# Seven half-size products in the first layer of a fused retention and MLP kernel, with two output buffers and two units cast sooner

## The chip, the cores and the metric

The kernel runs on one core of one Trainium2 chip. The metric is the device time of one launch in microseconds, lower is better. A version is compared with the kernel before in the same rounds on the same chip. The ratio given for it is the mean time of its fast runs over the mean time of the other's fast runs of the same rounds, so it isn't quite the ratio of the two medians that stand beside it.

## The reference

```python
def _attn_ref(q, k, v):                      # (8, 8, 576, 64) each, float32
    B, H, S, D_ = q.shape
    scores = (1.0 / np.sqrt(D_)) * np.matmul(q, k.transpose(0, 1, 3, 2))
    gamma = 1.0 - 2.0 ** (-5.0 - np.arange(H, dtype=np.float32))
    rel = np.arange(S)[:, None] - np.arange(S)[None, :]
    Dmat = np.where(rel >= 0, gamma[:, None, None] ** rel[None, :, :], 0.0)
    return np.matmul(scores * Dmat[None], v).astype(np.float32)

def _moe_ref(x, w_in, w_out):                # x (4608, 512), w_in (512, 2048), w_out (2048, 512)
    h = x @ w_in
    return (np.maximum(0.01 * h, h) @ w_out).astype(np.float32)
# reference: x is the attention output, heads side by side; the result is _moe_ref(x)
```

## The kernel before

Tokens come in 36 units of 128, and four units form a group of 512 (nine groups). A unit is loaded, cast (k on ScalarE, q and v with their decays on GpSimd), transposed by DMA, and turned into a piece of x by small matmuls ("scores", "outputs") and VectorE sums. A group then runs through two dense layers on TensorE. The second layer of groups 1 to 8 is already done as seven half-size products in place of eight, with the sums ("mix") on VectorE. The attention work of the next group is laid between the matmuls of this one. The code is shortened, and the comments are added for this text.

```python
    o_pool = ctx.enter_context(tc.tile_pool(name="op", bufs=3))      # output rows, 4 KB a partition each
    acc_pool = ctx.enter_context(tc.tile_pool(name="accp", bufs=4, space=PSUM))
    # ...
    def h_mm(hps, n, g, f, ts):
        for c in range(NP):                                          # NP = 4
            nc.tensor.matmul(out=hps[:, n, :], lhsT=w_in16[:, c, f * P : (f + 1) * P],
                             rhs=xT[g][:, c, ts], start=(c == 0), stop=(c == NP - 1))
    def h_block(g, f):                                               # one of 16 first-layer blocks of a group
        hps = acc_pool.tile([P, 1, TOK], FP, name="acc")             # TOK = 512
        h_mm(hps, 0, g, f, slice(0, TOK))
        leaky(g_tile(g)[:, f : f + 1, :], hps)                       # ScalarE
    def store(g, a, osb):
        nc.sync.dma_start(out=..., in_=osb)                          # SyncE's queue, as all later loads
    # second layer of group 0: wide(tb, part), one store half way, one at its end; of groups 1 to 8:
        plan = (
            ("p1", g_part(g, 0, 0), w_part(0, 0), True, lambda: keep("k1", "p1")),
            ("p1", g_part(g, 0, 1), w_part(1, 0), False, lambda: give(0, 0, "p1")),       # ScalarE
            ("p6", s[:, 1], w_mix[:, 1], True, lambda: keep("u2", "p6", "k1")),
            ("p5", s[:, 0], w_mix[:, 0], True, lambda: keep("v", "p5", "u2")),
            ("p7", g_part(g, 1, 0), w_mix[:, 2], True, lambda: give(1, 1, "p7", "v")),    # VectorE
            ("p5", g_part(g, 0, 0), w_part(1, 1), False, lambda: give(0, 1, "p5", "u2")), # VectorE
            ("p7", g_part(g, 1, 1), w_mix[:, 3], False, lambda: give(1, 0, "p7", "u2")),  # VectorE
        )
        # hooks after a product: 0 and 4 hold one step each
    # ...
    def burst(u, out=True):
        scores(u); outputs(u - 1)                                    # TensorE
        masks(u); state(u, 0); state(u, 1)                           # VectorE
        state_cast(u, pool_copy)                                     # GpSimd
        own(u - 1); add(u - 1)                                       # ScalarE, VectorE: a piece of x
    def ahead(u):
        cast_k(u)                                                    # ScalarE
        cast_q(u, nc.gpsimd); cast_v(u, nc.gpsimd)                   # GpSimd
        transpose_dma(u)                                             # SyncE's queue
    def step(u):
        burst(u); load(u + 4); ahead(u + 2)
```

Of the kernel before, what the change touches and what calls it, by code (L numbers as in the profile page):

```python
# [9 lines left out]
FP = mybir.dt.float32  # L10
F16 = mybir.dt.float16
MUL = mybir.AluOpType.mult
ADD = mybir.AluOpType.add
SUB = mybir.AluOpType.subtract
# [4 lines left out]
def kernel(  # L19
# [9 lines left out]
    nc = tc.nc  # L29
# [3 lines left out]
    P = 128  # L33
    CH = 64
    BLK = 256
    NP = H // 2
# [5 lines left out]
    HF, HN, HT = NF // 2, DM // 2, TOK // 2  # L42
# [11 lines left out]
    for w, at in enumerate(kinds):  # L54
        r = np.concatenate([CH * a + np.arange(CH) for a in at])[:, None] - BLK / 2
# [13 lines left out]
    const_pool = ctx.enter_context(tc.tile_pool(name="const", bufs=1))  # L69
# [3 lines left out]
    x_pool = ctx.enter_context(tc.tile_pool(name="xp", bufs=3))  # L73
    g_pool = ctx.enter_context(tc.tile_pool(name="gp", bufs=2))
    s_pool = ctx.enter_context(tc.tile_pool(name="sp", bufs=1))
    o_pool = ctx.enter_context(tc.tile_pool(name="op", bufs=3))
    m_pool = ctx.enter_context(tc.tile_pool(name="mp", bufs=1))
    sc_pool = ctx.enter_context(tc.tile_pool(name="scp", bufs=1, space=PSUM))
    ot_pool = ctx.enter_context(tc.tile_pool(name="otp", bufs=1, space=PSUM))
    acc_pool = ctx.enter_context(tc.tile_pool(name="accp", bufs=4, space=PSUM))  # L80
# [23 lines left out]
    w_in16 = const_pool.tile([P, NP, DFF], F16, name="w_in16")  # L104
    w_out16 = const_pool.tile([P, NF, DM], F16, name="w_out16")
    w_mix = const_pool.tile([P, 4, HF, HN], F16, name="w_mix")
    zst = const_pool.tile([P, NP, CH], F16, name="zst")
    idle = const_pool.tile([P, TOK], F16, name="idle")

    t32, qk16, v16, qkT, s16s, st16, sc_tiles, ot_tiles, xT = ({} for _ in range(9))  # L110
# [8 lines left out]
    def load(u, eng=None, after=None):  # L119
        for x in (1, 0, 2):  # L120
            t = ld_pool.tile([P, H, D], FP, name=f"t32_{x}")
            t32[u, x] = t
            c = 2 * u
            same = c % CB + 1 < CB
            e = eng[x] if isinstance(eng, dict) else eng or nc.sync
            engs = e if isinstance(e, tuple) else (e,)
            n = H // len(engs)
            for j, rows in ((0, P),) if same else ((0, CH), (1, CH)):
                b, w = (c + j) // CB, (c + j) % CB
                for i, e in enumerate(engs):  # L130
                    hs = slice(n * i, n * i + n)
                    d = e.dma_start(
                        out=t[CH * j : CH * j + rows, hs],
                        in_=(q, k, v)[x][b, hs, CH * w : CH * w + rows, :].rearrange(
                            "h t d -> t h d"
                        ),
                    )
                    if after is not None and (x in after or not isinstance(after, dict)):
                        behind(d, *(after[x] if isinstance(after, dict) else after))
                        after = None  # L140
                    last_load[u, x] = d
# [24 lines left out]
    def decay(u, x):  # L166
        w = kinds.index((place(2 * u), place(2 * u + 1)))
        return tab_sb[:, w, x, :].unsqueeze(2).to_broadcast([P, H, D])
# [5 lines left out]
    def cast_q(u, eng):  # L174
        eng.tensor_tensor(out=qk16[u][:, 0], in0=t32[u, 0], in1=decay(u, 0), op=MUL)  # L175

    def cast_v(u, eng):
        v16[u] = a_pool.tile([P, H, D], F16, name="v16")
        eng.tensor_tensor(out=v16[u], in0=t32[u, 2], in1=decay(u, 1), op=MUL)  # L179
# [54 lines left out]
    def masks(u):  # L234
        s16s[u] = b_pool.tile([P, 2, NP, CH], F16, name="s16")
        nc.vector.tensor_tensor(  # L236
            out=s16s[u],
            in0=sc_tiles[u][:, :, 0],
            in1=mask_sb.unsqueeze(1).unsqueeze(1).to_broadcast([P, 2, NP, CH]),
            op=MUL,  # L240
        )
# [3 lines left out]
    def state(u, j):  # L245

        if j == 0:
            s32s[u] = a_pool.tile([P, 2, NP, CH], FP, name="s32")
            st16[u] = a_pool.tile([P, 2, NP, CH], F16, name="st16")
        c = (2 * u + j) % CB  # L250
        if c == CB - 1:
            carry[0] = None
            return
        st = sc_tiles[u][:, j, 1]
        to = s32s[u][:, j]
        scaled = c % (BLK // CH) == BLK // CH - 1
        if carry[0] is None:
            nc.vector.tensor_copy(out=to, in_=st)
        elif not scaled:
            nc.vector.tensor_tensor(out=to, in0=st, in1=carry[0], op=ADD)  # L260
        else:
            tmp = m_pool.tile([P, NP, CH], FP, name="stmp")
            nc.vector.tensor_tensor(out=tmp, in0=st, in1=carry[0], op=ADD)
            nc.vector.tensor_tensor(  # L264
                out=to, in0=tmp,
                in1=gblk_sb.unsqueeze(2).to_broadcast([P, NP, CH]), op=MUL,
            )
        carry[0] = to
# [4 lines left out]
    def state_cast(u, copy, js=(0, 1)):  # L273
        js = [j for j in js if live(u, j)]
        if len(js) == 2:
            copy(out=st16[u], in_=s32s[u])  # L276
        else:
            for j in js:
                copy(out=st16[u][:, j], in_=s32s[u][:, j])  # L279
# [107 lines left out]
    def g_tile(g):  # L387
        if g not in g_t:
            g_t[g] = g_pool.tile([P, NF, TOK], F16, name="gt")
        return g_t[g]  # L390

    def leaky(out, in_):
        nc.scalar.activation(out=out, in_=in_, func=mybir.ActivationFunctionType.Lrelu)  # L393

    def h_block(g, f):
        hps = acc_pool.tile([P, 1, TOK], FP, name="acc")
        h_mm(hps, 0, g, f, slice(0, TOK))
        leaky(g_tile(g)[:, f : f + 1, :], hps)
# [8 lines left out]
    def h_unit(u, fb):  # L407
        g, t0 = u // 4, (u % 4) * P
        ts = slice(t0, t0 + P)
        hps = acc_pool.tile([P, 4, P], FP, name="acc")  # L410
        for n in range(4):
            h_mm(hps, n, g, 4 * fb + n, ts)
        leaky(g_tile(g)[:, 4 * fb : 4 * fb + 4, ts], hps)



# [29 lines left out]
    def mix_weights(n, x):  # L446
        fs = slice(x * HF // 2, (x + 1) * HF // 2)
        a, b = (
            (w_part(0, 1), w_part(0, 0)),
            (w_part(1, 1), w_mix[:, 0]),  # L450
            (w_part(1, 1), w_part(0, 1)),
            (w_part(1, 0), w_mix[:, 1]),
        )[n]
        nc.vector.tensor_tensor(out=w_mix[:, n, fs], in0=a[:, fs], in1=b[:, fs], op=SUB)
# [111 lines left out]
    pool_copy, act_copy, dve_copy = nc.gpsimd.tensor_copy, nc.scalar.copy, nc.vector.tensor_copy  # L566
# [82 lines left out]
    def halves(g, *items):  # L649
        for a, fb in items:  # L650
            h_half(g, a, fb)

    def cast_qv(u):
        cast_q(u, nc.vector)
        cast_v(u, nc.vector)
# [5 lines left out]
    def settle(u):  # L661
        state(u, 0)
        state_cast(u, dve_copy, (0,))
        masks(u)
        state(u, 1)
# [11 lines left out]
    def mixes(g, *ns):  # L677
        for n in ns:
            mix(g, n, 0)
            mix(g, n, 1)  # L680
# [16 lines left out]
    def ahead(u):  # L697

        if u >= NU:
            return  # L700
        cast_k(u)
        cast_q(u, nc.gpsimd)
        cast_v(u, nc.gpsimd)
        transpose_dma(u)
# [5 lines left out]
    def step(u):  # L710
        burst(u)
        fetch(u + 4)
        ahead(u + 2)
# [37 lines left out]
    turn(6, 0)  # L751
    h_unit(5, 0)
    scores(6)
    settle(6)
    cast_qv(7)
    h_unit(5, 1)
    turn(7, 1)
    halves(1, (0, 4))
# [15 lines left out]
    mix_weights(0, 0)  # L774
    mix_weights(0, 1)
    h_unit(7, 0)
    h_unit(7, 1)
    mix_weights(1, 0)
    mix_weights(1, 1)
    halves(1, (1, 4))  # L780
    load(10)
    ahead(8)
    mix_weights(2, 0)
    mix_weights(2, 1)
    halves(1, (1, 5), (1, 6))
    ahead(9)
    load(11)
    mix_weights(3, 0)
    mix_weights(3, 1)
    halves(1, (1, 7))  # L790

    def early(u, n):
        burst(u)
        ahead(n)
        load(n + 2)
# [4 lines left out]
        3: lambda: mixes(1, 1),  # L800
        4: lambda: (burst(8, False), ahead(11), load(13)),
        7: lambda: mixes(1, 2),
        9: lambda: early(9, 12),
    }
    for n in range(16):
# [1 line left out]
        if n in at:  # L807
            at[n]()
    burst(10)
    seven(1, {0: [lambda: early(11, 13)], 4: [lambda: early(12, 14)]})  # L810

    first = [f for i in range(4) for f in (i, i + HF)]
    second = [f for i in range(4, 8) for f in (i, i + HF)]
    for g in range(2, NG):
        more = g < NG - 1
        for n, f in enumerate(first + second):
            h_block(g, f)
            if more and n in (4, 12):
                step(4 * g + 5 + (n == 12))
            if n == 8:  # L820
                for m in range(3):
                    mix(g, m, 0)
        for m in range(3):
            mix(g, m, 1)
        seven(
            g,
            {0: [lambda: step(4 * g + 7)], 4: [lambda: step(4 * g + 8)]} if more else {},
            g == NG - 1,
        )

# [29 lines left out]
```

## Time and profile before

| | before |
|---|---|
| median of three runs | 289.74 us (288.94 to 289.91) |
| span of the profiled execution | 288.4 us |
| TensorE busy | 279.5 us, 97% |
| VectorE, ScalarE, GpSimd busy | 172.8, 143.7, 104.2 us |
| one steady group (groups 3 to 6) | 29.1 us, TensorE never idle |

In the profile a group of instructions is named by its line, engine, operation and its tile "out<-in". TensorE is what bounds this kernel, so its listed idle time, and what ended it, says whether another engine costs anything. In groups 2 to 8 of this kernel no such wait is listed.

### The profile page before, as it was taken

What the parts mean: (1) busy time and instruction counts of PE and PEld (TensorE: products, weight loads), DVE (VectorE), ACT (ScalarE), POOL (GpSimd) and SP (SyncE); (2) the same over time, 40 slices, a digit from 0 to 9 for tenths busy, and PEclk for the clock granted to TensorE, in tenths of its full rate; (3) what the DMA queues carried; (4) which work ended last, traced back from release to release, by engine and by line L of the source; (5) the groups of instructions that cost most, each with busy time, mean ns of one, the idle gap of its engine ahead of it and who ended that gap; (6) DMA issues with size and microseconds to landing.
All of it is one profiled execution on the core that took longest, in us unless ns stands there. A gap on an engine that the chain in (4) does not pass through costs nothing.

```text
span 288.4 us, 9432 instructions
## 1 busy us (share of the span) xinstructions
PE 279.5 (97%) x4111; PEld 190.5 (66%) x4111; DVE 172.8 (60%) x297; ACT 143.7 (50%) x254; POOL 104.2 (36%) x124
## 2 busy tenths in 40 slices
PE   8799999989999999999999999999999999999994
PEld 3478889545874587458745874587458844884583
DVE  2874787974664595459545863586368636740352
ACT  4676766623237632773277327732773176317610
POOL 8969503654333334332434333234225413000000
PEclk9999999999999999999999999999999999999999
DMA  8999999899999997976896669766986151012003
GB/s 221 297 228 203 293 207 213 187 195 212 217 254 283 210 212 164 277 148 148 183 256 152 146 153 285 148 144 152 283 159 147 45 177 39 3 65 84 0 2 145
DMA packets 131738, 50.01 MB, mean 173 GB/s; under 512 B 121264, under 2 KB 126000, under 8 KB 131696
## 3 DMA queue, kind: packets, MB, share of 16 engines
q1 hardware_dynamic: 125392, 39.59, 59.5%
q0 software_dynamic: 6016, 9.70, 15.0%
q8 instruction: 32, 0.52, 0.7%
q10 hardware_dynamic: 288, 0.11, 0.1%
q14 instruction: 10, 0.08, 0.1%
HBM read 36.81 MB, written 9.44 MB: 160 GB/s over the span
## 4 chain that ended last, share of the span: by engine, by line
PE 87%; DMA 6%; DVE 3%; ACT 2%; issue 1%; SPq 0%; POOL 0%; POOLq 0%
PE acc L379 41%; PE acc L493 34%; PE acc L429 3%; PE sc L218 3%; DMA t<-in_k_dram 2%; DMA t<-in_q_dram 2%; PE ot L294 2%; DMA qkT<-qk 2%; PE sc L227 1%; PE ot L305 1%; PE acc L200 1%; ACT qkT L207 1%; PE acc L327 1%; DVE s L236 0%; DVE xT L366 0%
## 5 line engine op out<-in xcount | busy, mean ns | idle before, releaser
L379 PE MATMUL acc<-xT,w_in 128*128 128x512 f16 (+2 forms) x768 | 131.0, 326 | 0.3 <-ACT xT L347 0.2
L393 ACT ACTIVATE gt<-acc 128x512 f16<-128x512 f32 x144 | 85.9, 597 | 56.9 <-PE acc L379 55.5
L379 PEld LDWEIGHTS <-w_in 128*128 128x128 f16 x768 | 68.2, 98 | 51.7 <-issue 0.2
L493 PEld LDWEIGHTS <-gt 128*128 128x128 f16 x640 | 61.8, 98 | 9.1
L236 DVE TENSOR_TENSOR s<-sc,cs 128x512 f16<-128x512 f32 x34 | 23.3, 686 | 39.7 <-PE sc L227 39.7
L493 PE MATMUL acc<-w_out,gt 128*128 128x256 f16 x384 | 45.9, 273 | 0.2
L276 POOL CAST st<-s 128x512 f16<-128x512 f32 x21 | 12.8, 609 | 89.7 <-DVE s L260 56.3
L361 ACT COPY own<-ot 128x512 f32<-128x512 f32 x33 | 19.3, 585 | 42.8 <-PE ot L305 35.6
L175 POOL TENSOR_TENSOR qk<-t,cs 128x512 f16<-128x512 f32 x28 | 29.9, 1067 | 19.4 <-DMA t<-in_q_dram 19.0
L473 DVE TENSOR_TENSOR mix<-gt 128x1024 f16<-128x1024 f16 x16 | 15.7, 984 | 28.8 <-ACT gt L393 28.8
L179 POOL TENSOR_TENSOR v<-t,cs 128x512 f16<-128x512 f32 x28 | 31.9, 1139 | 1.2 <-DMA t<-in_v_dram 1.2
L493 PE MATMUL acc<-w_mix,gt 128*128 128x256 f16 x256 | 30.6, 273 | 0.0
L493 PE MATMUL acc<-w_mix,mix 128*128 128x256 f16 x256 | 29.6, 273 | 0.0
L493 PEld LDWEIGHTS <-mix 128*128 128x128 f16 x256 | 25.0, 98 | 3.1 <-DVE mix L473 0.2
L172 ACT CAST qk<-t 128x512 f16<-128x512 f32 x36 | 22.3, 621 | 8.7 <-DMA t<-in_k_dram 8.7
L366 DVE TENSOR_TENSOR xT<-ot,own 128x512 f16<-128x512 f32 x33 | 22.6, 684 | 4.9 <-ACT own L361 4.9
L260 DVE TENSOR_TENSOR s<-sc,s 128x256 f32<-128x256 f32 x37 | 15.5, 419 | 2.1 <-PE sc L227 1.4
L218 PEld LDWEIGHTS <-qkT 64*64 64x64 f16 x576 | 7.8, 107 | 13.2 <-issue 10.4
L519 DVE TENSOR_TENSOR osb<-acc,u 128x512 f32<-128x512 f32 (+1 forms) x17 | 11.2, 657 | 7.9 <-PE acc L493 7.9
L473 DVE TENSOR_TENSOR mix<-mix,gt 128x1024 f16<-128x1024 f16 x16 | 14.8, 932 | 0.5
L279 POOL CAST st<-s 128x256 f16<-128x256 f32 x7 | 3.2, 453 | 31.3 <-DVE s L264 19.4
L429 PE MATMUL acc<-w_out,gt 128*128 128x512 f16 x64 | 14.3, 379 | 0.0
(57 smaller groups left out, 234.2 us busy)
## 6 DMA issues: line engine op xcount, KB each, us to landing
out_dram<-osb SPq DMA_DIRECT2D x17, 512.0 KB, 3.6
t<-in_k_dram SPq DMA_DIRECT2D x27, 256.0 KB, 4.0
t<-in_q_dram SPq DMA_DIRECT2D x26, 256.0 KB, 4.1
t<-in_v_dram SPq DMA_DIRECT2D x25, 256.0 KB, 4.9
w_in<-in_moe_w_in_dram POOLq DMA_DIRECT2D x8, 256.0 KB, 6.8
w_out<-in_moe_w_out_dram POOLq DMA_DIRECT2D x4, 512.0 KB, 10.2
t<-in_v_dram POOLq DMA_DIRECT2D x7, 256.0 KB, 5.6
t<-in_q_dram POOLq DMA_DIRECT2D x6, 256.0 KB, 5.8
```

The lines of the kernel that those rows point to most:

```text
L172: nc.scalar.copy(out=qk16[u][:, 1], in_=t32[u, 1])
L175: eng.tensor_tensor(out=qk16[u][:, 0], in0=t32[u, 0], in1=decay(u, 0), op=MUL)
L179: eng.tensor_tensor(out=v16[u], in0=t32[u, 2], in1=decay(u, 1), op=MUL)
L218: nc.tensor.matmul(out=a[half(j), g, 0, p, :], lhsT=qkT[u][half(g), 1, p, half(j)], rhs=qkT[u][half(g), 0, p, half(j)], start=True, stop=T ...
L236: nc.vector.tensor_tensor(out=s16s[u], in0=sc_tiles[u][:, :, 0], in1=mask_sb.unsqueeze(1).unsqueeze(1).to_broadcast([P, 2, NP, CH]), op=MUL,)
L361: nc.scalar.copy(out=owns[u], in_=ot_tiles[u][:, :, 0:NP].rearrange("q j c t -> q c j t"))
L366: nc.vector.tensor_tensor(out=x_of(u).rearrange("q (c g) t -> q c g t", g=2), in0=ot_tiles[u][:, :, NP : 2 * NP].rearrange("q g (c j) t -> ...
L379: nc.tensor.matmul(out=hps[:, n, :], lhsT=w_in16[:, c, f * P : (f + 1) * P], rhs=xT[g][:, c, ts], start=(c == 0), stop=(c == NP - 1),)
L393: nc.scalar.activation(out=out, in_=in_, func=mybir.ActivationFunctionType.Lrelu)
L429: nc.tensor.matmul(out=ys[tb], lhsT=g_t[0][:, f, tb * P : (tb + 1) * P], rhs=w_out16[:, f, :], start=(f == 0), stop=(f == NF - 1),)
L473: nc.vector.tensor_tensor(out=z[:, fs], in0=a[:, fs], in1=b[:, fs], op=op)
L493: nc.tensor.matmul(out=r[name][tb][:, 0, :] if apart else r[name][0][:, tb, :], lhsT=lhs[:, f, tb * P : (tb + 1) * P], rhs=rhs[:, f, :], s ...
```

## The change

The intent: in groups 2 to 8, four of the 16 first-layer blocks are computed by seven products of half size in place of eight, as the second layer does already. The sums of w_in are made once, those of x once a group (VectorE, two 16-bit SBUF inputs each). The new tiles need SBUF, so the output pool goes from three buffers to two. Apart from that, the casts and transposes of units 8 and 9 move up in the start, and unit 7's q cast goes ahead of unit 6's second state. The diff is shortened.

```diff
-    o_pool = ctx.enter_context(tc.tile_pool(name="op", bufs=3))
+    o_pool = ctx.enter_context(tc.tile_pool(name="op", bufs=2))
+    w_sum = const_pool.tile([P, 4, NP // 2, 2 * P], F16, name="w_sum")
 ...
+    def sum_x(g):
+        x_sums[g] = t = s_pool.tile([P, 4, NP // 2, HT], F16, name="x_sum")
+        for n, (a, b) in enumerate(( (x_sub(g, 0, 1), x_sub(g, 0, 0)), (x_sub(g, 1, 1), t[:, 0]),
+                                     (x_sub(g, 1, 1), x_sub(g, 0, 1)), (x_sub(g, 1, 0), t[:, 1]) )):
+            nc.vector.tensor_tensor(out=t[:, n], in0=a, in1=b, op=SUB)
+
+    # ... h_seven's own helpers are left out
+    def h_seven(g, fill):                # product: 2 x 2 matmuls of 256 columns; plus: VectorE; give: ScalarE
+        product("p1", w_sub(0, 0), x_sub(g, 0, 0), True)
+        r["k1"] = m_pool.tile([P, 2, HT], FP, name="k1")
+        nc.scalar.copy(out=r["k1"], in_=r["p1"])
+        h_block(g, fill[0])
+        product("p1", w_sub(0, 1), x_sub(g, 1, 0), False)
+        give(0, 0, "p1")
+        product("p6", w_sum[:, 1], t[:, 1], True)
+        plus("u2", "p6", "k1")
+        product("p5", w_sum[:, 0], t[:, 0], True)
+        plus("v", "p5", "u2")
+        h_block(g, fill[1])
+        product("p7", w_sum[:, 2], t[:, 2], True)
+        plus("h4", "p7", "v")
+        product("p5", w_sum[:, 3], x_sub(g, 1, 1), False)
+        plus("h5", "p5", "u2")
+        give(1, 1, "h4")
+        h_block(g, fill[2])
+        give(0, 1, "h5")
+        product("p7", w_sub(1, 1), t[:, 3], False)
+        plus("h6", "p7", "u2")
+        give(1, 0, "h6")
 ... (start)
-    settle(6)
-    cast_qv(7)
+    state(6, 0); state_cast(6, dve_copy, (0,)); masks(6)
+    cast_q(7, nc.vector); state(6, 1); cast_v(7, nc.vector)
 ...
     h_unit(7, 0)
+    ahead(8)
+    load(10)
     h_unit(7, 1)
 ...
-    load(10)
-    ahead(8)
 ... (second layer of group 0, then of groups 1 to 7)
+        12: lambda: [sum_w_in(n) for n in range(4)],
-    seven(1, {0: [lambda: early(11, 13)], 4: [lambda: early(12, 14)]})
+    seven(1, {0: [lambda: early(11, 13)], 4: [lambda: early(12, 14)], 5: [lambda: sum_x(2)]})
 ... (each group from 2 on)
-        for n, f in enumerate(first + second):
+        h_seven(g, rest[:3])
+        for n, f in enumerate(rest[3:]):
 ...
-            {0: [lambda: step(4 * g + 7)], 4: [lambda: step(4 * g + 8)]} if more else {},
+            {0: [lambda: step(4 * g + 7)], 4: [lambda: step(4 * g + 8)], 5: [lambda: sum_x(g + 1)]} if more else {},
```

More of the change, by code (lines that the diff above doesn't have):

```diff
@@ L413, in h_unit, with w_sub, x_sub, sum_w_in @@
         leaky(g_tile(g)[:, 4 * fb : 4 * fb + 4, ts], hps)
+    def w_sub(i, j):
+        return w_in16[:, 2 * j : 2 * j + 2, i * HF * P : i * HF * P + 2 * P]
+    def x_sub(g, j, k):
+        return xT[g][:, 2 * j : 2 * j + 2, k * HT : (k + 1) * HT]
+    def sum_w_in(n):
+        a, b, op = (
+            (w_sub(1, 0), w_sub(1, 1), ADD),
+            (w_sum[:, 0], w_sub(0, 0), SUB),
+            (w_sub(0, 0), w_sub(1, 0), SUB),
+            (w_sub(0, 1), w_sum[:, 1], SUB),
+        )[n]
+        nc.vector.tensor_tensor(out=w_sum[:, n], in0=a, in1=b, op=op)
@@ new lines, with product, plus, give @@
+    x_sums = {}
+    def sum_x(g):
+        x_sums[g] = t = s_pool.tile([P, 4, NP // 2, HT], F16, name="x_sum")
+        for n, (a, b) in enumerate(
+            (
+                (x_sub(g, 0, 1), x_sub(g, 0, 0)),
+                (x_sub(g, 1, 1), t[:, 0]),
+                (x_sub(g, 1, 1), x_sub(g, 0, 1)),
+                (x_sub(g, 1, 0), t[:, 1]),
+            )
+        ):
+            nc.vector.tensor_tensor(out=t[:, n], in0=a, in1=b, op=SUB)
+    def h_seven(g, fill):
+        r = {}
+        t = x_sums[g]
+        def product(name, lhs, rhs, fresh):
+            if fresh:
+                r[name] = acc_pool.tile([P, 2, HT], FP, name="acc")
+            for n in range(2):
+                for c in range(NP // 2):
+                    nc.tensor.matmul(
+                        out=r[name][:, n, :],
+                        lhsT=lhs[:, c, n * P : (n + 1) * P],
+                        rhs=rhs[:, c, :],
+                        start=fresh and n == 0 and c == 0,
+                        stop=c == NP // 2 - 1,
+                        skip_group_check=True,
+                    )
+        def plus(name, a, b):
+            r[name] = m_pool.tile([P, 2, HT], FP, name=name)
+            nc.vector.tensor_tensor(out=r[name], in0=r[a], in1=r[b], op=ADD)
+        def give(i, k, name):
+            leaky(g_tile(g)[:, i * HF : i * HF + 2, k * HT : (k + 1) * HT], r[name])
+        product("p1", w_sub(0, 0), x_sub(g, 0, 0), True)
[19 more added lines that the diff above has]
+        give(1, 0, "h6")
@@ L753 @@
     scores(6)
-    settle(6)
-    cast_qv(7)
+    state(6, 0)
+    state_cast(6, dve_copy, (0,))
+    masks(6)
+    cast_q(7, nc.vector)
+    state(6, 1)
+    cast_v(7, nc.vector)
     h_unit(5, 1)
@@ L779 @@
     mix_weights(1, 1)
-    halves(1, (1, 4))
-    load(10)
-    ahead(8)
+    halves(1, (1, 4), (1, 5))
     mix_weights(2, 0)
     mix_weights(2, 1)
-    halves(1, (1, 5), (1, 6))
     ahead(9)
     load(11)
+    halves(1, (1, 6))
     mix_weights(3, 0)
@@ L809 @@
     burst(10)
-    seven(1, {0: [lambda: early(11, 13)], 4: [lambda: early(12, 14)]})
-    first = [f for i in range(4) for f in (i, i + HF)]
-    second = [f for i in range(4, 8) for f in (i, i + HF)]
+    seven(1, {0: [lambda: early(11, 13)], 4: [lambda: early(12, 14)], 5: [lambda: sum_x(2)]})
+    rest = [f for i in range(2, HF) for f in (i, i + HF)]
     for g in range(2, NG):
         more = g < NG - 1
-        for n, f in enumerate(first + second):
+        h_seven(g, rest[:3])
+        for n, f in enumerate(rest[3:]):
             h_block(g, f)
-            if more and n in (4, 12):
-                step(4 * g + 5 + (n == 12))
-            if n == 8:
+            if more and n in (0, 6):
+                step(4 * g + 5 + (n == 6))
+            if n == 3:
                 for m in range(3):
```

## The prediction

> **What bounds the kernel now.** I read the page's busy times first, then the table of stages (busy time of each engine in stretches that I chose), then the chain that ended last, then TensorE's waits.
>
> ```profile
> PE 279.5 (97%) x4111; PEld 190.5 (66%) x4111; DVE 172.8 (60%) x297; ACT 143.7 (50%) x254; POOL 104.2 (36%) x124
> ...
> PEclk9999999999999999999999999999999999999999
> ```
>
> TensorE is busy 97% of the span and at its full clock throughout, so only shorter TensorE work or fewer TensorE waits can help. The stage table, for one steady group (times of PE, PEld, DVE, ACT, POOL) and for the last group:
>
> ```profile
> 200.50:229.60 29.10, 29.07 (x434) 19.35 (x433) 17.77 (x29) 14.94 (x26) 11.14 (x14) 1.00 0.68 157
> ...
> 258.50:288.40 29.90, 26.22 (x177) 16.93 (x174) 9.55 (x16) 10.72 (x18) 0.00 (x0) 1.00 0.19 70
> ```
>
> In a steady group of 29.10 us TensorE has no idle time to speak of (29.07 busy); VectorE has 11.3 us to spare, ScalarE 14.2. So inside groups 2 to 8, which hold the new code, a removed matmul is worth what it takes on TensorE, unless a new wait eats it. The chain (start, duration, what) gives the rates:
>
> ```profile
> 99.44 1.75 PE acc L493 x16
> ...
> 258.55 13.81 PE acc L379 x64
> 272.36 12.37 PE acc L493 x112
> ```
>
> L379 is the first layer with 512 columns: 13.81 / 64 = 215.8 ns each. L493 is the half-size second-layer product with 256 columns: 1.75 / 16 = 109.4 ns, 12.37 / 112 = 110.4 ns. A half-size matmul thus costs 50.7% of a full one, not less than half, and its weight load (98 ns) hides beside it.
>
> TensorE's listed waits add up to under 5 us, nearly all in the first 60 us. The one that the change aims at:
>
> ```profile
> PE sc L218 <- DMA qkT<-qk: 1.2, 1, 1.2
> ```
>
> That is unit 8's scores, waiting for its transposing DMA until 58.52 us. The chain puts the transpose at 54.05 us, landing 4.43 us later, and names POOL's cast at 53.21 before it. But that cast is unit 9's. The timeline shows unit 8 ready earlier: its q cast ran on POOL from 48.24 to 49.45 and its k cast on ACT from 50.94 to 51.55. What held it is the order of the SyncE queue: the change's code shows load(10) ahead of ahead(8), and the timeline has those three loads at 49.93, 52.32 and 53.09, the transposes right behind.
>
> **What the Trainium skill says.** "TensorE: Matmul & The Clock Gate", section "Back-to-back issue gap", gives 518 cycles for 512 columns and 262 for 256 at 2.4 GHz: 215.8 and 109.2 ns. The trace agrees (215.8, 109.4). "VectorE: DVE Perf Modes", in its section on the TRN2 errata, has (N+151)/0.96 ns for a two-tensor fp32 operation: 691 ns for 512 elements; the trace has 692 (L507) and 657 to 686 in similar groups. Two 16-bit elements a cycle make 1024 elements 691 ns too, and the trace has 684 to 693 for undisturbed L473. "SBUF — State Buffer", section "Who interferes with whom", says that a VectorE instruction with two SBUF inputs contends with GpSimd's SBUF reads, one blocking the other for the whole instruction. The trace agrees, and it is what I fear most:
>
> ```profile
> 47.27 1.28 DVE L454 TENSOR_TENSOR w_mix<-w_out 128x1024 f16<-128x1024 f16 x2
> ...
> 48.24 1.21 POOL L175 TENSOR_TENSOR qk<-t,cs 128x512 f16<-128x512 f32 x1 [14.31 <-DMA t<-in_q_dram]
> 48.47 2.98 DVE L454 TENSOR_TENSOR w_mix<-w_out,w_mix 128x1024 f16<-128x1024 f16 x2
> ...
> 49.42 1.48 POOL L179 TENSOR_TENSOR v<-t,cs 128x512 f16<-128x512 f32 x1
> ```
>
> Two such operations take 1.28 us alone and 2.98 beside POOL's casts: each waits for one whole POOL cast, in turns. VectorE operations with one PSUM input (L519, L236) stay at 0.68 to 0.69 beside POOL.
>
> **The change part by part.** *Removed, per group of 2 to 8:* four first-layer blocks, 16 matmuls of 512 columns: 16 x 215.8 = 3.45 us. *Added:* seven products of 2 x 2 matmuls of 256 columns, 28 x 109.4 = 3.06 us. Saved 0.39 us a group, 2.7 us in seven groups. This is small because only a quarter of one layer is treated, and seven replace eight.
>
> *ScalarE:* four activations before, four after (three now read SBUF), plus one copy of 0.59 us; it has 14 us to spare. *VectorE:* five sums from PSUM of 0.69 us (about 0.60 from start to start) and four 16-bit operations of 512 elements for the sums of x; by the skill's formula (256+151)/0.96 = 424 ns, an estimate, and some 0.35 us apart. Together about 4.5 us a group, so 17.8 becomes some 22 of 28.7: not a bound by volume. The four sums of w_in run once in the second layer of group 0, where VectorE idles 3.85 us (66 to 69.75): hidden.
>
> *Inside the seven products* I laid out TensorE from the group's start G: first product to G+0.44, a filling block to 1.30, its second half to 1.74, p6 to 2.17, p5 to 2.61, a block to 3.47, p7 to 3.91. The sums u2 and v end about 0.9 and 1.5 us after p6 ends, before p5's second use (1.74 after); ScalarE's copy of p1 (0.2 + 0.59 us) fits under the 0.86 of the filling block with 0.07 to spare. So the fillings are enough if VectorE comes to u2 on time.
>
> *It may not.* The sums of the next group's x are queued on VectorE in the preceding second layer, between its last two output sums (L519). These are, in the timeline of one such place:
>
> ```profile
> 228.09 0.68 DVE L519 TENSOR_TENSOR osb<-acc,u 128x512 f32<-128x512 f32 x1
> 228.31 1.04 POOL L175 TENSOR_TENSOR qk<-t,cs 128x512 f16<-128x512 f32 x1
> 229.31 1.04 POOL L179 TENSOR_TENSOR v<-t,cs 128x512 f16<-128x512 f32 x1
> ...
> 229.74 0.69 DVE L519 TENSOR_TENSOR osb<-acc,u 128x512 f32<-128x512 f32 x1 [0.97 <-PE acc L493]
> ```
>
> POOL's two casts lie just where the x sums would go, 228.7 on. In turns: the first x sum waits until 229.3 and ends at 229.7; POOL's v cast runs to 230.75; then the other three to 231.8, and the last output sum to 232.45. It frees the fourth accumulator, and in a rotation of four p5 takes that one, wanted at G+2.17 = 231.87: TensorE would stand some 0.6 us. The same working at the other five boundaries with POOL casts (starting groups 2 to 6) gives 0.95, 0.5, 0.5, 1.05 and 1.0. The boundary before group 8 has no cast. Sum 4.6 us if it is all so, more than the products save.
>
> *Start.* Unit 8's k cast comes one activation earlier and its transpose ahead of load(10): about 50 us in place of 54.05, landing near 54.5 where 57.3 is needed. That removes the 1.2 us. The swap of q's cast ahead of unit 6's second state removes TensorE's 0.4 us at L200, but the chain there is VectorE without a gap from 38.91 to 43.5, whose work stays the same; I count nothing. Two output buffers in place of three: stores land 3.6 us after issue and a buffer comes up again after several us, no wait.
>
> *Sum:* 289.74 - 2.7 - 1.2 = 285.8 without the new wait, 290.4 with all of it. I give the wait 60%: 289.74 - 3.9 + 0.6 x 4.6 = 288.6.
>
> **The rivals.** (a) *All hidden:* 285.8 us. For it: the fillings and VectorE's idle time; whoever placed them had waits in mind. Against: the casts at each boundary. (b) *VectorE's queue becomes the limit at the group's start* through turns with POOL: 290.4, or 292 if semaphores add 0.1 us at every product. For it: the 2.98 us above; against: the turns are seen only with operations twice as long. (c) *The transposes gain nothing* because loads of units 10 and 11, now later by some 2 us, hold ACT's k cast or a later score: then 1.2 us more. Unit 10 is needed only at 69.3, so 15%. (d) *256-column matmuls between 512-column blocks run slower:* against it, 1.75 per 16 right after a switch.
>
> **Range and chances.** Between (a) and (b) with 0.3 us on one side and 0.9 on the other: 285.5 to 291.3. Faster by 2% needs 284.0, more than all savings together: 0.03. Slower by 2% needs 295.5, twice the feared wait: 0.03.
>
> **What the changed profile would show.** First-layer matmuls of 256 columns at 109 ns; the steady group at 28.7 us with PE fully busy if (a), or 29.1 to 29.8 with a wait of TensorE before p5 released by L519 on VectorE if (b), with x sums of 0.42 us alone and up to 1.4 beside POOL; no such wait in group 8. The wait of L218 for qkT gone and the transpose near 50 us. Wrong would make it: an accumulator taken in another order, POOL's casts coming elsewhere, or a wait that I missed in an exact copy six times over.

## More of the kernel before

The experiments ran in three batches on three chips, so versions of different batches are compared by their ratios.

Line numbers differ between the two kernels: the first layer's blocks are L379 before and L380 after, the second layer's products L493 and L573, VectorE's output sums L519 and L599.

One view of this profile turned out to matter more than any that the prediction shows, SyncE's queue at the end of group 0. Each line has start, duration and what was issued (the shortened part holds transposes and loads alone); its only two stores between 60 and 80 us are among them:

```profile
62.62 1.05 SPq L132 DMA_DIRECT2D t<-in_k_dram  x1
63.78 0.53 SPq L132 DMA_DIRECT2D t<-in_q_dram  x1
64.40 1.23 SPq L132 DMA_DIRECT2D t<-in_v_dram  x1
65.81 1.65 SPq L183 DMA_TRANSPOSE qkT<-qk  x1
67.55 1.39 SPq L132 DMA_DIRECT2D t<-in_k_dram  x2
69.04 1.27 SPq L132 DMA_DIRECT2D t<-in_q_dram  x2
70.40 2.14 SPq L132 DMA_DIRECT2D t<-in_v_dram  x2
72.64 0.58 SPq L419 DMA_DIRECT2D out_dram<-osb  x1
...
78.05 0.78 SPq L419 DMA_DIRECT2D out_dram<-osb  x1
```

And ScalarE's copies that completed what these stores write, in the same stretch:

```profile
61.95 0.58 ACT L439 COPY osb<-acc 128x512 f32<-128x512 f32 x1
...
69.35 0.58 ACT L439 COPY osb<-acc 128x512 f32<-128x512 f32 x1 [1.43 <-PE acc L429]
```

The first half is complete at 62.53 us and leaves at 72.64, the second at 69.93 and 78.05. The stores stand 10.1 and 8.1 us in the queue, behind input loads and transposes: the issues in the seven lines ahead of the first add up to 9.3 us. With three buffers no engine waits for it.

## The result

| | before | after |
|---|---|---|
| median of six runs | 289.64 us | 294.25 us (293.21 to 295.54) |
| ratio, 95% interval | | 1.0169 (1.0139 to 1.0200) |
| span of the profiled execution | 288.4 us | 292.2 us |

The change is 1.7% slower, and 294.25 lies above the predicted range of 285.5 to 291.3. Two of the six runs had a granted clock of 0.993 and 0.994 and took 295.5 and 295.4; the other four, at full clock as far as recorded, took 293.2 to 294.3.

The busy times after, in the form of the prediction's first fence:

```profile
PE 278.3 (95%) x4195; PEld 198.4 (68%) x4195; DVE 224.1 (77%) x364; ACT 145.3 (50%) x261; POOL 110.5 (38%) x124
```

TensorE does 1.2 us less and the span is 3.8 us longer, so TensorE now waits. What it waits for from 60 us on (engine and tile, releaser: total, times, longest, in us). The kernel before has only the last kind there, with the same 0.2:

```profile
PE acc L457 <- DVE osb L599: 2.1, 5, 0.7
PE acc L573 <- DVE osb L599: 1.3, 1, 1.3
PE acc L457 <- DVE x_sum L445: 1.2, 1, 1.2
PE acc L457 <- DVE v L468: 0.5, 1, 0.5
PE acc L573 <- ACT k L585: 0.4, 1, 0.4
PE ot L295 <- DVE xT L367: 0.2, 1, 0.2
```

L457 is a half-size product of the first layer. Five times it waits for VectorE's output sum, as rival (b) said. The waits in the lines below it are of other kinds and come once each. Who was VectorE itself waiting for? Its list of waits, and ScalarE's, name something new, an output DMA:

```profile
DVE osb L599 <- DMA out_dram<-osb: 4.1, 1, 4.1
ACT osb L597 <- DMA out_dram<-osb: 3.9, 1, 3.9
```

Both are in group 1's second layer, at 81.72 and 76.69 us: its two output tiles want the two buffers that group 0's stores still hold. Those stores leave at 71.37 and 77.38 us, no earlier than they used to in relation to the rest:

```profile
71.37 0.58 SPq L499 DMA_DIRECT2D out_dram<-osb  x1
...
77.38 0.76 SPq L499 DMA_DIRECT2D out_dram<-osb  x1
```

The table shows where the span went. It has the start of group 2 (its first first-layer matmul in the timeline) and the length of groups 2 to 7 from one such start to the next, for the two kernels and for the three versions that the next section tries:

| us | group 2 starts | 2 | 3 | 4 | 5 | 6 | 7 |
|---|---|---|---|---|---|---|---|
| before | 83.97 | 29.11 | 29.12 | 29.11 | 29.11 | 29.12 | 28.84 |
| after | 84.21 | 31.06 | 29.20 | 29.19 | 29.72 | 29.89 | 29.21 |
| after, three buffers | 82.69 | 29.63 | 29.19 | 29.20 | 29.72 | 29.66 | 28.93 |
| after, GpSimd's casts earlier | 84.80 | 29.85 | 28.84 | 28.84 | 28.85 | 29.19 | 28.58 |
| after, both | 83.36 | 28.84 | 28.85 | 28.85 | 28.84 | 28.85 | 28.57 |

And this is one boundary between groups in the changed kernel, the start of group 7, from the timeline (start, duration, engine, what; idle time before and its end in brackets):

```profile
231.83 0.68 DVE L599 TENSOR_TENSOR osb<-acc,u 128x512 f32<-128x512 f32 x1
232.04 1.04 POOL L176 TENSOR_TENSOR qk<-t,cs 128x512 f16<-128x512 f32 x1
232.42 0.94 DVE L445 TENSOR_TENSOR x_sum<-xT 128x512 f16<-128x512 f16 x1
233.04 1.23 POOL L180 TENSOR_TENSOR v<-t,cs 128x512 f16<-128x512 f32 x1
...
233.40 1.15 DVE L445 TENSOR_TENSOR x_sum<-xT,x_sum 128x512 f16<-128x512 f16 x1
...
234.47 0.41 DVE L445 TENSOR_TENSOR x_sum<-xT 128x512 f16<-128x512 f16 x1
...
234.81 0.41 DVE L445 TENSOR_TENSOR x_sum<-xT,x_sum 128x512 f16<-128x512 f16 x1
...
235.14 0.68 DVE L599 TENSOR_TENSOR osb<-acc,u 128x512 f32<-128x512 f32 x1
235.87 0.60 PE L457 MATMUL acc<-x_sum,w_sum 128*128 128x256 f16 x4 [0.25 <-DVE osb L599]
```

The first x sum stands 0.94 us, 0.42 of its own and the rest nearly until GpSimd's q cast ends (233.08); then the v cast waits for it and takes 1.23 in place of 1.04; then the second x sum waits for the v cast and takes 1.15; the last two take 0.41 each. The output sum comes behind all four and ends at 235.82, and p5 starts at 235.87. TensorE's previous product began at 235.03 and needs 0.44, so p5 is 0.40 us late. The trace lists only 0.25, because the end of a matmul in it lies later than the start of the next (0.27 us long, 0.109 apart).

### The profile page after: what moved, and what is told of

It is laid out like the page before. It is cut to its first block, busy times and chain, and to the rows that moved or that the text cites. A ratio compares the mean times of both kernels' runs of the same rounds, so it can differ in the third digit from the quotient of the medians.

```text
span 292.2 us, 9709 instructions
## 1 busy us (share of the span) xinstructions
PE 278.3 (95%) x4195; PEld 198.4 (68%) x4195; DVE 224.1 (77%) x364; ACT 145.3 (50%) x261; POOL 110.5 (38%) x124
## 4 chain that ended last, share of the span: by engine, by line
PE 63%; DVE 17%; SPq 6%; DMA 5%; issue 3%; POOL 3%; ACT 2%; DVEq 0%; POOLq 0%; ACTq 0%
PE acc L380 29%; PE acc L573 24%; DVE x_sum L445 6%; DMA t<-in_q_dram 5%; PE acc L457 4%; DVE osb L599 4%; SPq L133 3%; SPq L184 2%; DVE xT L367 2%; PE sc L219 1%; DVE s L237 1%; POOL v L180 1%; ACT k L585 1%; PE ot L295 1%; DVE s L261 1%
## 5 line engine op out<-in xcount | busy, mean ns | idle before, releaser
L380 PE MATMUL acc<-xT,w_in 128*128 128x512 f16 (+2 forms) x656 | 110.3, 317 | 0.4 <-DVE xT L367 0.2
L394 ACT ACTIVATE gt<-acc 128x512 f16<-128x512 f32 x123 | 72.4, 597 | 33.1 <-PE acc L380 32.3
L380 PEld LDWEIGHTS <-w_in 128*128 128x128 f16 x656 | 57.3, 98 | 34.2 <-issue 0.5
L176 POOL TENSOR_TENSOR qk<-t,cs 128x512 f16<-128x512 f32 x28 | 32.1, 1148 | 18.9 <-DMA t<-in_q_dram 17.3
L180 POOL TENSOR_TENSOR v<-t,cs 128x512 f16<-128x512 f32 x28 | 36.1, 1290 | 0.0
L553 DVE TENSOR_TENSOR mix<-mix,gt 128x1024 f16<-128x1024 f16 x16 | 19.9, 1248 | 0.5
L457 PEld LDWEIGHTS <-w_sum 128*128 128x128 f16 x112 | 10.7, 97 | 8.4 <-issue 3.9
L394 ACT ACTIVATE gt<-h 128x512 f16<-128x512 f32 x21 | 13.2, 627 | 4.9 <-DVE h L468 4.6
L457 PE MATMUL acc<-x_sum,w_sum 128*128 128x256 f16 x84 | 12.3, 272 | 3.2 <-DVE osb L599 2.1
```

What stands on the lines that cost most here:

```text
L176: eng.tensor_tensor(out=qk16[u][:, 0], in0=t32[u, 0], in1=decay(u, 0), op=MUL)
L180: eng.tensor_tensor(out=v16[u], in0=t32[u, 2], in1=decay(u, 1), op=MUL)
L394: nc.scalar.activation(out=out, in_=in_, func=mybir.ActivationFunctionType.Lrelu)
L457: nc.tensor.matmul(out=r[name][:, n, :], lhsT=lhs[:, c, n * P : (n + 1) * P], rhs=rhs[:, c, :], start=fresh and n == 0 and c == 0, stop=c ...
L553: nc.vector.tensor_tensor(out=z[:, fs], in0=a[:, fs], in1=b[:, fs], op=op)
```

## The experiments

**Two output buffers alone, in the kernel before.**

```diff
-    o_pool = ctx.enter_context(tc.tile_pool(name="op", bufs=3))
+    o_pool = ctx.enter_context(tc.tile_pool(name="op", bufs=2))
```

> The kernel before with nothing changed but two output buffers in place of three. Theory A (the missing third buffer is a cost of its own: the stores of group 0 wait in SyncE's queue behind input loads until 71 and 77 us, so group 1's output sums find no buffer): VectorE waits over 2 us for an out DMA near 80 us, TensorE stalls some 0.8 to 1.3 us before the last product of group 1's second layer, and the time is 290.4 to 291.2 against 289.6. Theory B (all of the loss is the x sums' turns with GpSimd): no wait, 289.6 within 0.3.

Measured: 292.21 us against 289.69, ratio 1.0082 (1.0044 to 1.0119). TensorE's waits from 60 us on:

```profile
PE acc L493 <- DVE osb L519: 2.0, 1, 2.0
PE acc L379 <- DVE xT L366: 0.5, 1, 0.5
PE ot L294 <- DVE xT L366: 0.2, 1, 0.2
```

VectorE waits 4.8 us for an output DMA. Group 2 starts at 85.74 us, where another execution of the kernel before, 0.1 us ahead of this one at 57 us, had 82.76. So the missing buffer costs 2.4 us by the ratio, and 2.9 in these two traces, without any other part of the change. Theory A holds, and its size of 0.8 to 1.3 us was too small: I had counted the last product's wait alone, and too short, and had left out the first-layer matmul that waits for x behind it.

**Three output buffers in the changed kernel** (h6 shares h4's tile, which makes room).

```diff
-    o_pool = ctx.enter_context(tc.tile_pool(name="op", bufs=2))
+    o_pool = ctx.enter_context(tc.tile_pool(name="op", bufs=3))
 ...
-            r[name] = m_pool.tile([P, 2, HT], FP, name=name)
+            r[name] = m_pool.tile([P, 2, HT], FP, name="h4" if name == "h6" else name)
```

> The changed kernel with three output buffers again (space made by letting h6 use h4's buffer). Theory A (buffer and turns both cost): group 2 starts at about 82.8 us in place of 84.2, the 1.3, 1.15 and 0.54 us waits around it shrink to one of about 0.8, the later groups keep their waits of 0.4 to 0.8; the time falls by 3.0 to about 291.3. Theory B (turns alone): no change, 294.2. Theory C (it was only the late start of VectorE that also shifted the later groups): under 289.5.

Measured: 290.47 us against 289.69, ratio 1.0022 (0.9987 to 1.0058). Theory A holds, and the fall is larger than its 3.0: 3.8 us between the medians. Group 2 starts at 82.69, and from 60 us on these two waits are left:

```profile
PE acc L457 <- DVE osb L599: 2.7, 6, 0.7
PE ot L295 <- DVE xT L367: 0.2, 1, 0.2
```

**Group 0's two stores from ScalarE's queue**, with two buffers as in the change.

```diff
-        nc.sync.dma_start(
+        (nc.scalar if g == 0 else nc.sync).dma_start(
```

> The changed kernel with two output buffers, but group 0's two stores issued from ScalarE's queue in place of SyncE's. Theory A (the buffers come late because the stores stand behind input loads in SyncE's queue): VectorE's wait for the out DMA near 78 us is gone, as fast as with three buffers, 290.2 to 290.9. Rival (two buffers are too few however early the stores go, or the transfers themselves take over 8 us): a wait stays and the time is above 292.5.

Measured: 291.23 us against 289.13, ratio 1.0067 (1.0055 to 1.0079); the other kernel's median is lower in these rounds. The stores leave at 61.96 and 69.02 us, no engine waits for an output DMA any more, and group 2 starts at 83.00:

```profile
61.96 0.43 ACTq L499 DMA_DIRECT2D out_dram<-osb  x1
69.02 0.41 ACTq L499 DMA_DIRECT2D out_dram<-osb  x1
```

So two buffers are enough to end the wait for the output DMA. What costs is the place of the stores in SyncE's queue. The time is 0.3 us above the range expected, and the ratio is a little above that of the version with three buffers (1.0022); their intervals just overlap. The two traces show a rest too: group 8 starts at 259.57 against 259.02. Group 2 starts 0.31 us later, most of it a wait for x of 0.43 us in place of 0.17: a VectorE sum ahead of x takes 0.70 us beside a GpSimd cast in place of 0.42. Group 6 takes 29.89 us in place of 29.66, as in the change, because the sum u2 there starts 0.48 us after the output sum's end; why stays open.

**GpSimd's casts earlier.** In the second step of each second layer, the casts of the next unit go ahead of the state cast in GpSimd's queue, into time in which GpSimd waited for VectorE. The same edit also puts that unit's k cast ahead of the step's copy on ScalarE, and its transpose ahead of the next load on SyncE. Two buffers as in the change.

```diff
+    def cast_first(u, n):
+        ahead(n); burst(u); fetch(u + 4)
 ...
-            4: [lambda: step(4 * g + 8)], 5: [lambda: sum_x(g + 1)]
+            4: [lambda: cast_first(4 * g + 8, 4 * g + 10)], 5: [lambda: sum_x(g + 1)]
```

> The changed kernel, but in the second step within each second layer GpSimd's q and v casts of the next unit stand before the state cast in its queue, so that they run in its idle time and not beside the x sums. Still two output buffers. Theory A: the x sums take 0.41 us each, TensorE's waits before p5 in groups 3 to 7 (0.41, 0.41, 0.82, 0.81, 0.41 counting the modelled ends) vanish, the time falls by 2.5 to 3.5 to about 291.3. Rival (VectorE's queue is too long there even without GpSimd: 1.4 us of x sums and 0.6 of output sum reach G+2.1): the waits stay at 0.2 to 0.5 each and the time falls by under 1.5.

Measured: 290.72 us against 289.69, ratio 1.0028 (0.9989 to 1.0066). Theory A holds: the x sums take 0.42 us each (0.64 and 0.73 on average in the change), and groups 3 to 5 take 28.84 or 28.85 us. Left are the buffer's wait, 2.2 us in group 1, and two waits for v:

```profile
PE acc L573 <- DVE osb L599: 2.2, 1, 2.2
PE acc L457 <- DVE v L468: 0.8, 2, 0.5
PE ot L295 <- DVE xT L367: 0.2, 1, 0.2
```

The rival, that VectorE's queue is too long there even alone, falls: with the same queue on VectorE the waits on the output sum in groups 2 to 7 are gone. The first wait for v is group 2's, behind the buffer; the second, 0.25 us in group 6, isn't explained, and the version with both cures hasn't got it.

**The same move of casts in the kernel before, as a control.**

> Control: the kernel before with only GpSimd's casts ahead of the state cast in the same steps. There are no x sums to collide with, TensorE waits for nothing there, so 289.6 within 0.4. If it were over 1 us faster, the gain of the same edit in the changed kernel would not show that the turns with the x sums cost time.

Measured: 289.34 us against 289.13, ratio 1.0005 (0.9993 to 1.0018). The move, on all three engines, is worth nothing where there are no x sums, so what it is worth in the changed kernel is their collision.

**Three buffers, and the x sums behind the last output sum.** Only the place of the sums changes (hook 6 for hook 5); GpSimd's casts stay as in the change.

```diff
-            4: [lambda: step(4 * g + 8)], 5: [lambda: sum_x(g + 1)]
+            4: [lambda: step(4 * g + 8)], 6: [lambda: sum_x(g + 1)]
```

> Three output buffers, and the x sums behind the last output sum of the second layer in place of in front of it; GpSimd's casts as in the change. Theory A (TensorE waits for the fourth accumulator, which that output sum frees, not for the x sums): the wait before p5 on the output sum is gone, a smaller wait on x sums or u2 of at most 0.3 us takes its place, 287 to 288.5. Rival (the x sums themselves are late): waits on x sums of 0.5 us or more, 289.5 to 291.

Measured: 288.54 us against 289.13, ratio 0.9982 (0.9966 to 0.9997), at the upper end of the range expected. No wait for the output sum is left; two of 0.2 us for x sums come in its place. So what p5 stood for was the accumulator that the output sum frees, as theory A had it. It is slower than the next version; in the trace groups 2, 5 and 6 take 29.16, 29.25 and 29.19 us, and in 5 and 6 TensorE waits for x sums that end late.

**Both cures.**

> The changed kernel with three output buffers and with GpSimd's casts ahead in each second layer's second step. If the two causes are separate and complete: group 2 starts at 82.7 us, groups of 28.8 us, no TensorE wait over 0.3 us after 60 us; the three-buffer version (290.47) less 3.1 to 3.7, so 286.8 to 287.4, some 0.8 to 1% faster than before. If something else costs too (the half-size products themselves slower than counted), it stays above 288.5.

Measured: 287.15 us against 289.13, ratio 0.9932 (0.9920 to 0.9945). Groups 2 to 6 take 28.84 or 28.85 us, and from 60 us on TensorE waits as little as in the kernel before:

```profile
PE ot L295 <- DVE xT L367: 0.2, 1, 0.2
```

**The start.** Three experiments bear on it. First the kernel before with the start's reordering alone:

```diff
-    load(10)
-    ahead(8)
+    ahead(8)          # two blocks sooner, then load(10)
     # and ahead(9) one block sooner; cast_q(7) ahead of state(6, 1)
```

> The kernel before with only the start's reordering (units 8 and 9 cast and transposed sooner, and the order of casts at unit 7). Theory A: L218's wait of 1.2 us for qkT is gone, everything after shifts by 1.2 to 1.35 us, 288.3 to 288.5. Rival (the later loads of units 10 and 11 take it back): 289.6 within 0.3. No gain from the unit 7 part: group 1's first matmul on unit 6 at 43.5 us as before.

Measured: 289.01 us against 289.69, ratio 0.9967 (0.9928 to 1.0006), which decides little. Unit 8's transpose leaves at 50.01 us, as counted, but does anything wait for it otherwise? The version with both cures, with the old start put back:

> The version with three buffers and early casts, with the start put back as in the kernel before: what is left is the half-size products with their sums, without either of the two costs. If groups of 28.85 us in place of 29.11 are all the gain, 7 x 0.26 = 1.8 us, so 0.994 of the time before (287.4 to 287.9), and the start is then worth no more than 0.5 us. If the start is worth the 1.2 us counted in the prediction, it stands above 288.2.

Measured: 287.02 us against 289.70, ratio 0.9916 (0.9893 to 0.9939). It is no slower than with the new start, and 0.4 us below the range expected of it. The kernel before, unchanged, looked at twice more:

> The kernel before, unchanged, one more look. Two other profiles with the same start (two output buffers; early casts) show no wait of L218 for qkT, the first profile shows 1.18 us. If that wait depends on the execution, it differs here from 1.18, anywhere from 0 to 1.2 us; if it belongs to the kernel, it is 1.0 to 1.3 again.

> The same kernel and the same question as the run before this one, for one more sample of the wait of L218 for qkT: 0 to 1.2 us if it depends on the execution, 1.0 to 1.3 if it belongs to the kernel.

In both, the wait of L218 for qkT is absent. The matmuls in question, in the first of them:

```profile
57.32 0.32 PE L218 MATMUL sc<-qkT 64*64 64x64 f16 x16
```

and in the profile that the prediction was made from:

```profile
58.52 0.32 PE L218 MATMUL sc<-qkT 64*64 64x64 f16 x16 [1.18 <-DMA qkT<-qk]
```

Over the six executions that I have with the old start, the wait is 1.18, 0, 0, 0 (two buffers), 0 (control) and 0.50 us (both cures). The transposes left at 54.05 us in the first and 54.52 in the last, and at 52.80 to 53.59 in the others. The start's queue runs a little later in some executions, and in these six TensorE waits only then. With the new start the transpose leaves at 49.6 to 50.5 us and no trace has the wait; a gain in the other executions isn't shown.

## Why the prediction was wrong

**Which step failed.** "Two output buffers in place of three: stores land 3.6 us after issue and a buffer comes up again after several us, no wait." The 3.6 us is the median of all stores (these two landed 5.2 and 4.2 us after issue in the change), and it is the wrong interval to count: a buffer isn't free a transfer's time after it is filled, but after it is filled, has stood in the queue, and has been transferred. In this queue group 0's halves stood 10.1 and 8.1 us, and that was to be read in the profile before. The two-buffer experiment shows 2.4 us from that cause alone, and the stores from ScalarE's queue show that the standing is it. None of the prediction's rivals contained it.

**The wait at the group's start: right in mechanism, below the size counted.** Rival (b), turns with GpSimd in front of the output sum that frees p5's accumulator, is shown by the trace and by three experiments. I had counted 0.95, 0.5, 0.5, 1.05, 1.0 and 0.6 us for groups 2 to 7, 4.6 in all. With three buffers the groups exceed those of the version without collisions by 0.79, 0.34, 0.35, 0.88, 0.81 and 0.36, 3.5 in all. The pattern is the same, and the sizes are 0.15 to 0.24 us smaller. Two errors of the working partly cancel. It took group 7's start as 229.70 from the chain, where the timeline has 229.54, which makes the count 0.16 too small. And it let each instruction begin at the listed end of the one that it waits for. In the boundary shown above a sum needs 0.42 us and the two that wait end at 233.36 and 234.55, so they began some 0.14 us before the casts' listed ends of 233.08 and 234.27, and the v cast likewise; over three hand-overs that is 0.4. These last figures are estimates from the undisturbed durations. (The 292 us in rival (b) doesn't follow from its own terms either: 0.1 us at each of 49 products is 4.9 us, not 1.6.) My weight of 60% on the wait looks low, since the trace before already had all the parts.

**The two together cost more than each.** In the changed kernel groups 2 to 7 exceed 28.85 us (28.57 in group 7) by 5.5 us, 1.9 more than with three buffers. Most of that is group 2: VectorE comes 4 us late from its buffer and has the x sums next, so TensorE waits for x sums (1.2) and v (0.5), which no other group has. Group 6 adds 0.23, of open cause, and group 7 adds 0.28 with a wait for ScalarE's copy. By the traces: two buffers cost 1.4 us before group 2 (84.21 against 82.8) and 1.9 after it (0.5 of this in groups 6 and 7, where a tie to the wait for the buffer isn't shown), the turns 3.5, and the products give 1.6 in six groups; 1.4 + 1.9 + 3.5 - 1.6 = 5.2. Group 8 starts at 262.48 us, against 257.17 in the look at the kernel before that had no wait for qkT: 5.3. In the runs the change is 1.69% of 289.6, 4.9 us.

**The products: mis-sized.** I counted 0.39 us a group, and the groups without collisions are 0.26 or 0.27 shorter than before (28.84 against 29.11). From the first product to the first burst, 28 half-size matmuls and four blocks come to 6.52 us by the rates used; one such stretch takes 6.68, where the kernel before exceeds the same count by 0.08 over five blocks. So some 0.08 us of it lies in the products' stretch, most of it a small wait of p5 for v; the rest I didn't locate.

**The start: mis-sized, 1.2 counted and about 0 found**, because one profile was taken for the kernel. The prediction's reading of that wait (the order of SyncE's queue) fits the traces with the new order, where the transpose leaves some 4 us sooner; that the wait is there in each run does not hold. That cast_q(7) sooner gains nothing was right: scores and first layer of unit 6 follow at the same time, now waiting for VectorE's copies instead (0.3 us).

**Right as well:** group 8, before which there is no cast, has no wait; the sums of w_in hide; k1's copy fits; VectorE is not a bound by volume; matmuls of 256 columns between blocks of 512 keep their 109 ns.

## What to carry to other kernels

Before a pool loses a buffer, look up in the trace when its transfers *leave*, not how long they take: a store in an in-order queue behind input loads holds its buffer for the queue's delay. When new VectorE work with two SBUF inputs is placed, look at what GpSimd does at that moment, and keep in front of it whatever frees an accumulator; here reordering GpSimd's own queue cost nothing and took the collision away. And before a wait in the start is counted as a gain, look at it in more than one execution.

The version with both cures is 0.7% faster than the kernel before (0.9932; 0.9916 with the old start), the best seen here.

## What the Trainium skill lacked or had wrong

- "DMA: Bandwidth & Descriptors", section "Issuing engines are not separate DMA queues", says that issuing from several engines saves only the sequencer's time to initiate a DMA, which is usually small relative to the DMA itself. Here it was not: the issues ahead of a store in SyncE's queue added up to 9.3 us, where the store itself landed in 4.6. Moving two stores to ScalarE's queue let them leave 9.4 and 8.4 us sooner (61.96 and 69.02 against 71.37 and 77.38) and took the ratio from 1.0169 to 1.0067. The page lacks that a DMA stands behind the earlier ones on its issuing engine and holds its buffer meanwhile.
- "SBUF — State Buffer", section "Who interferes with whom", has the lock between VectorE with two SBUF inputs and GpSimd right. It lacks what happens between two queues that both have such work: they take turns, instruction by instruction, so a 0.42 us sum lasted 0.94 and 1.15 us, and a GpSimd cast of 1.04 us lasted 1.23.
- "Perfetto Trace Analysis", on the Tensor Engine's instructions, says that a matmul's end is estimated. It lacks the consequence for waits: the listed idle time before a 256-column matmul was 0.25 us where its start was 0.40 late.
